# Cluster attention and two gated layers on one core: the product of p and v in one run every second iteration, the fill's steps in the other iterations

## The chip, the cores and the metric

One core of a Trainium2 chip runs the whole program. The metric is the device time of one execution in microseconds (us); the median of the runs counts.

## The reference, cut to what is computed

Attention with 2 batches, 8 heads, 768 tokens and a head dimension of 64; a key counts for a query only if both have the same nearest centroid (of 16). Its output passes through two feed-forward blocks.

```python
q_assign = np.argmax(np.einsum('bhsd,hcd->bhsc', q_n, c_n), axis=-1)
k_assign = np.argmax(np.einsum('bhsd,hcd->bhsc', k_n, c_n), axis=-1)
mask = q_assign[:, :, :, None] == k_assign[:, :, None, :]
scores = np.where(mask, scale * np.matmul(q, k.transpose(0, 1, 3, 2)), -1000000000.0)
attn = np.exp(scores - np.max(scores, axis=-1, keepdims=True))
attn = attn / (np.sum(attn, axis=-1, keepdims=True) + 1e-09)
x = np.matmul(attn, v)                       # (1536, 512) after the heads are joined
x = ((x @ w1) * (x @ w2)) @ w3 @ w_out       # 512 -> 1024 -> 1024 -> 512
h = x @ w_in                                 # 512 -> 2048
out = (np.maximum(h, 0.0) + alpha * np.minimum(h, 0.0)) @ w_out2
```

## The kernel before, in words

The attention is cut into 96 "units": 16 heads (b, h) times 6 tiles of 128 queries. Two neighbouring units form a pair g (48 of them). A software pipeline written out by hand (the loop of L710) runs one iteration per unit; iteration i holds steps of several units:

- `emit_T(i - 4)`: six transposes of the normalised p of unit i-4 on TensorE, into the two buffers of the PSUM tag "t" (L497);
- `emit_S(i + 1)`: four products that make the scores of unit i+1, two of 128 rows (L457) and two of 80 rows that add the mask (L458);
- `emit_x`: takes the finished output o of a pair out of PSUM, half by ScalarE (L527), half by VectorE (L528); `emit_r`: reciprocals of the row sums of a pair on VectorE (L479, L480); `emit_norm(i - 2)`: p times the reciprocal on GpSimd (L483);
- `emit_evac(i - 4)`: the transposes out of PSUM into the tile pt, three by ScalarE (L504), three by VectorE (L505);
- `emit_max(i + 1)`: row maxima on VectorE (L465); `emit_exp(i)`: the exponential on ScalarE (L472);
- `h_split`: once per unit u of six iterations the operands of the next head are prepared: at i = 6u three operations on GpSimd (L416, L417, L421), then a chain of transfers on the SP queue (L427, L429, L431, and the mask rows mk, L435 and L436); the first score product of the next head waits for them;
- one step of the `fill` (a generator of other work). In the first half the fill prepares the masks of the remaining heads (its products are called ja, jb, jc, jd and je); from iteration 56 a step is 12 products of 384 columns (called l1a and l1b) of the first feed-forward layer for batch 0. With a fill step go steps of the weight conversion (`w_goal`): three operations on VectorE (L181, L182, L185), then a cast on ScalarE (L226) and a subtraction on GpSimd (L227). Before the change a fill step runs in every iteration below 24, between 41 and 55 and from 96 on, and otherwise in even iterations;
- `emit_PV(g, part)`: the product of p and v of pair g. The two units of the pair go to two column halves of the array (tile positions (0, 0) and (0, 64)), each 64 columns wide, while all other products of the loop but ja use the full 128 columns. Three of the six key tiles are done in iteration 2g+6, three in 2g+7; in the trace each half is a run of 12 matmul records (each fp32 product is two records), that is 6 records side by side on the two halves. The PSUM tag "o" has one buffer, so the product of the next pair waits until `emit_x` has emptied it.

After the loop come the rest of the first layer for batch 0, then batch 1, and the remaining layers.

On every engine the order of instructions is that of the code (`manual_schedule`), and each engine waits in order.

Of the kernel before, what the change touches and what calls it, by code (L numbers as in the profile page):

```python
# [17 lines left out]
P = 128  # L18
NT = S // P
# [9 lines left out]
def kernel(  # L29
# [221 lines left out]
    def pst(tag, shape, name, bufs=1):  # L251
        return ps.tile(shape, F32, tag=tag, name=name, bufs=bufs)
# [151 lines left out]
    def h_split(u, j):  # L404

        if u >= B * H:
            return
        b, h = divmod(u, H)
        if j == 0:
            ST[u] = st_tile(f"st{u}")  # L410
        s, r = ST[u], hraw.get(u)
        f = f32(s)
        pool = u % 2 == 1 or 0 < u < 9
        if j == 0:
            if pool:
                nc.gpsimd.tensor_scalar(out=r, in0=r, scalar1=qsc, scalar2=1.0, op0=ALU.mult, op1=ALU.mult)  # L416
            nc.gpsimd.tensor_scalar(  # L417
                out=s[:, 3], in0=r, scalar1=1.0 if pool else qsc, scalar2=1.0, op0=ALU.mult, op1=ALU.mult
            )
            if pool:  # L420
                nc.gpsimd.tensor_tensor(out=s[:, 1], in0=r, in1=f[:, 3], op=ALU.subtract)  # L421
            else:
                nc.vector.scalar_tensor_tensor(
                    out=s[:, 1], in0=r, scalar=qsc, in1=f[:, 3], op0=ALU.mult, op1=ALU.subtract
                )
        elif j == 1:
            nc.sync.dma_start(out=f[0:64, 0:4:2], in_=f[64:128, 3:4].to_broadcast([64, 2, S]))  # L427
        elif j == 2:
            nc.sync.dma_start(out=f[64:128, 0], in_=f[64:128, 1])  # L429
        elif j == 3:  # L430
            nc.sync.dma_start(out=f[64:128, 1], in_=f[0:64, 3])  # L431
        elif j == 4:
            mk = MK[b, h // 4].rearrange("p a b -> p (a b)")
            hl = h % 4
            nc.sync.dma_start(out=f[64:80, 2], in_=mk[16 * hl : 16 * hl + 16])  # L435
            nc.sync.dma_start(out=f[64:80, 3], in_=mk[64 + 16 * hl : 64 + 16 * hl + 16])  # L436
        else:
            hraw.pop(u)
            h_load(u + 1)


    NU = B * H * NT
    scp, pt, sums, pth, ob, XR = {}, {}, {}, {}, {}, {}

    def unit(i):
        return i // NT, i % NT

    def emit_S(i):
        if i >= NU:
            return  # L450
        u, qt = unit(i)
        s = ST[u]
        t = pst("s", [P, 2, 512], f"s{i}", bufs=2)
        q = slice(qt * P, qt * P + P)
        for a in range(2):
            ks = slice(a * HS, a * HS + HS)
            nc.tensor.matmul(t[:, a, 0:HS], lhsT=s[:, 0, q], rhs=s[:, 1, ks], start=True, stop=False)  # L457
            nc.tensor.matmul(t[:, a, 0:HS], lhsT=s[0:80, 2, q], rhs=s[0:80, 3, ks], start=False, stop=True)  # L458
        scp[i] = t
# [3 lines left out]
    def emit_max(i):  # L463
        m = ap.tile([P, 1], F32, tag="nmax", bufs=3, name=f"nm{i}")
        nc.vector.tensor_reduce(out=m, in_=scp[i][:, :, 0:HS], op=ALU.max, axis=AX.XY, negate=True)  # L465
        nmax[i] = m

    def emit_exp(i):
        if i % 2 == 0:
            sums[i // 2] = ap.tile([P, 2], F32, tag="sums", bufs=3, name=f"su{i}")  # L470
        p = ap.tile([P, S], F32, tag="p", bufs=6, name=f"p{i}")
        nc.scalar.activation(  # L472
            out=p.rearrange("p (a k) -> p a k", a=2), in_=scp.pop(i)[:, :, 0:HS], func=AF.Exp,
            bias=nmax.pop(i), scale=1.0, accum_out=sums[i // 2][:, i % 2 : i % 2 + 1],
        )
        pt[i] = p

    def emit_r(g):
        nc.vector.tensor_scalar(out=sums[g], in0=sums[g], scalar1=1e-9, scalar2=None, op0=ALU.add)  # L479
        nc.vector.reciprocal(out=sums[g], in_=sums[g])  # L480

    def emit_norm(i):
        nc.gpsimd.tensor_scalar(  # L483
            out=pt[i], in0=pt[i], scalar1=sums[i // 2][:, i % 2 : i % 2 + 1], scalar2=1.0, op0=ALU.mult, op1=ALU.mult
        )
# [3 lines left out]
    def emit_T(i):  # L489
        g, j = divmod(i, 2)  # L490
        if j == 0:
            pth[g] = ap.tile([P, NT, 256], F32, tag="pth", bufs=3, name=f"pt{g}")
        for a in range(2):
            t = pst("t", [P, 3, P], f"t{i}{a}", bufs=2)
            for k in range(3):
                kt = 3 * a + k
                nc.tensor.transpose(t[:, k], pt[i][:, kt * P : kt * P + P], ident)  # L497
            tps[i, a] = t
        pt.pop(i)

    def emit_evac(i):
        g, j = divmod(i, 2)
        q = slice(j * P, j * P + P)
        nc.scalar.copy(out=pth[g][:, 0:3, q], in_=tps.pop((i, 0)))  # L504
        nc.vector.tensor_copy(pth[g][:, 3:6, q], tps.pop((i, 1)))  # L505

    def emit_PV(g, part):

        u, qt = unit(2 * g)
        if part == 0:  # L510
            ob[g] = pst("o", [P, P], f"o{g}")
        v = VS[u // 2]
        for kt in range(3 * part, 3 * part + 3):
            for j in range(2):
                nc.tensor.matmul(  # L515
                    ob[g][64 * j : 64 * j + 64], lhsT=v[:, u % 2, kt], rhs=pth[g][:, kt, j * P : j * P + P],
                    start=(kt == 0), stop=(kt == NT - 1), tile_position=(0, 64 * j),
                )

    def emit_x(g):  # L520
        u, qt = unit(2 * g)
        o = ob.pop(g)
        p = u // 2
        if u % 2 == 0 and qt == 0:
            XR[p] = cp.tile([P, S], F32, tag=f"xr{p % 4}", name=f"xr{p}")
        mine = slice(0, 64) if u % 2 == 0 else slice(64, 128)
        nc.scalar.copy(out=XR[p][mine, qt * P : qt * P + P], in_=o[0:64])  # L527
        nc.vector.tensor_copy(XR[p][mine, qt * P + P : qt * P + 256], o[64:128])  # L528
        pth.pop(g)
# [17 lines left out]
    def x_split(b, p, a):  # L547
        if b not in XS:
            XS[b] = cp.tile([P, 8 * S], F32, tag="wox", name=f"xs{b}").bitcast(F32R).rearrange("p (t k s) -> p t k s", t=2, k=4)
        r = XR[4 * b + p]  # L550
        s = slice(a * HS, a * HS + HS)
        nc.scalar.copy(out=XS[b][:, 0, p, s], in_=r[:, s])
        pool = a if b == 1 else 1 - a
        (nc.gpsimd if pool else nc.vector).tensor_tensor(out=XS[b][:, 1, p, s], in0=r[:, s], in1=f32(XS[b][:, 0, p, s]), op=ALU.subtract)
# [25 lines left out]
    with tc.manual_schedule():  # L580
# [126 lines left out]
        LT = 4  # L707
        L1_B, L1_D = 16, 24
        NUH = NU // 2
        for i in range(NU + 9):  # L710
            if 0 <= i - LT < NU:
                emit_T(i - LT)
            if i + 1 < NU:
                emit_S(i + 1)

            g2 = i - 8
            if g2 >= 0 and g2 % 2 == 0 and g2 // 2 < NU // 2:
                emit_x(g2 // 2)
            if i >= 2 and i % 2 == 0 and i // 2 - 1 < NU // 2:
                emit_r(i // 2 - 1)  # L720
            if 0 <= i - 2 < NU:
                emit_norm(i - 2)
            if 0 <= i - LT < NU:
                emit_evac(i - LT)
            if i + 1 < NU:
                emit_max(i + 1)
            if i < NU:
                emit_exp(i)
                u, j = unit(i)
                for k in ((0,), (1, 2), (3,), (4,), (5,), ())[j]:  # L730
                    h_split(u + 1, k)
            if i >= NU or i % 2 == 0 or i < 24 or 40 < i < 56:
                if fill_at[0] < (L1_B if i < NU else L1_D):
                    if next(fill) is not None:
                        fill_at[0] += 1
            if NUH + 4 <= i < NUH + 8:
                x_split(0, i - NUH - 4, 0)
                x_split(0, i - NUH - 4, 1)
                xdone.append(i)
            if i == NU - 1:  # L740
                late.append(i)
                for k in range(2):
                    w = st_tile(f"wo{k}").rearrange("p a n -> p (a n)").rearrange("p (g t n) -> p g t n", g=3, t=2)
                    for g in range(3):
                        WO[3 * k + g] = w[:, g, 0], w[:, g, 1]
            if i >= NU - 1:
                w_goal(at["wo", 0, 3, 0])

            k = i - 6
            if k >= 0 and k // 2 < NU // 2:  # L750
                emit_PV(k // 2, k % 2)
                if k % 12 == 11:
                    v_load(k // 12 + 2)
        pscope.close()

# [178 lines left out]
```

## Time and profile before

| what | us |
|---|---|
| runs before | 808.74, 809.0, 2352.5; median 809.0 |
| the profiled execution's own time | 809.13 |
| its span, first to last instruction | 807.0 |
| busy in it: PE (matmul) | 769.3 (95%) |
| busy in it: DVE | 496.5 (62%) |
| busy in it: ACT | 393.7 (49%) |
| busy in it: POOL | 244.7 (30%) |

One of the three runs lies far off and does not move the median. The span is 2.1 us shorter than the execution's own time. PE, DVE, ACT, POOL and SP are TensorE, VectorE, ScalarE, GpSimd and the engine that issues transfers. A matmul's duration in the trace is its latency: neighbouring records overlap, so what a product costs is the distance between starts.

### The profile page before, as it was taken

Reading aid. Unit: us, or ns where it says so; the run is one execution under the profiler, and the core shown is the slowest. Engines: PE = TensorE matmul, PEld = TensorE weight load, DVE = VectorE, ACT = ScalarE, POOL = GpSimd, SP = SyncE. Lnnn points to the kernel's source line nnn. Section 1 sums busy time; section 2 is a strip of 40 time slices with the busy share of each in tenths; the row PEclk is TensorE's granted clock in tenths of the full one; section 3 lists DMA queues with packets and bytes.
Section 4 is the critical chain, followed back from the end, with each engine's and each line's share of the span. In section 5 each row is a group of like instructions: output and inputs, shape, how many; then the busy total and the mean of one; then the engine's idle time right before and its main releaser. Section 6 shows DMA issues by size and latency. Waiting matters only on the chain.

```text
span 807.0 us, 13411 instructions
## 1 busy us (share of the span) xinstructions
PE 769.3 (95%) x5073; PEld 679.6 (84%) x5073; DVE 496.5 (62%) x836; ACT 393.7 (49%) x836; POOL 244.7 (30%) x222
## 2 busy tenths in 40 slices
PE   4799999799999999969999999999999999999998
PEld 2667888678888888959998899999999878999996
DVE  3866888987878777785545599334456663323222
ACT  5677766665555564543233345334544554323232
POOL 0465456566464534243222243001112220000000
PEclk9999999999999999979999999999999999999999
DMA  7555344545545517546444498025665738333332
GB/s 250 175 160 175 76 107 101 139 98 158 161 147 139 165 55 213 188 172 225 161 137 160 154 310 276 39 79 167 212 191 187 225 115 287 131 120 121 126 131 78
DMA packets 38863, 127.31 MB, mean 158 GB/s; under 512 B 5168, under 2 KB 5296, under 8 KB 38800
## 3 DMA queue, kind: packets, MB, share of 16 engines
q1 hardware_dynamic: 38800, 126.46, 50.0%
q8 instruction: 40, 0.66, 0.3%
q14 instruction: 23, 0.19, 0.1%
HBM read 84.08 MB, written 28.31 MB: 139 GB/s over the span
## 4 chain that ended last, share of the span: by engine, by line
PE 84%; DVE 6%; ACT 3%; issue 3%; DMA 2%; POOL 1%; SPq 1%; POOLq 0%; ACTq 0%; DVEq 0%
PE o L515 9%; PE t L497 8%; PE l L246 8%; PE l L244 8%; PE l L245 7%; PE acc L246 5%; PE acc L245 5%; PE acc L244 5%; PE s L457 4%; PE s L458 4%; PE l1a L245 3%; PE l1a L244 3%; PE l1a L246 3%; PE l1b L244 2%; PE l1b L245 2%
## 5 line engine op out<-in xcount | busy, mean ns | idle before, releaser
L227 POOL TENSOR_TENSOR wh<-wt,wh 128x512 fp32r<-128x512 f32 x64 | 86.5, 1352 | 239.0 <-DVE g L852 119.6
L483 POOL TENSOR_SCALAR p<-p,su 128x768 f32<-128x768 f32 x96 | 91.3, 958 | 125.8 <-DVE su L480 64.2
L848 DVE SCALAR_TENSOR_TENSOR gr<-gr,alp 128x384 f32<-128x384 f32 x64 | 41.7, 651 | 107.3 <-ACT gr L847 107.3
L465 DVE TENSOR_REDUCE nm<-s 128x1 f32<-128x768 f32 x96 | 91.5, 953 | 9.9 <-PE s L458 6.3
L472 ACT ACTIVATE p<-s,nm 128x768 f32<-128x768 f32 x96 | 87.0, 906 | 6.2 <-DVE nm L465 6.2
L515 PE MATMUL o<-pt,vs 128*64 128x128 f32 x1152 | 84.6, 282 | 5.3 <-DVE xr L528 5.3
L497 PE MATMUL t<-cst,p 128*128 128x128 f32 x576 | 85.2, 283 | 1.7 <-DVE pt L505 1.7
L515 PEld LDWEIGHTS o<-pt,vs 128*64 128x64 f32 x1152 | 61.4, 137 | 29.4 <-issue 18.3
L457 PE MATMUL s<-st 128*128 128x384 f32 x192 | 74.4, 387 | 3.4 <-ACT p L472 3.3
L497 PEld LDWEIGHTS t<-cst,p 128*128 128x128 f32 x576 | 61.6, 141 | 18.8 <-issue 13.1
L246 PE MATMUL acc<-wh,g 128*128 128x512 f32 x192 | 75.3, 392 | 0.0
L244 PE MATMUL acc<-wh,g 128*128 128x512 f32 x192 | 74.8, 390 | 0.6 <-ACT os L872 0.6
L245 PE MATMUL acc<-wh,g 128*128 128x512 f32 x192 | 75.3, 392 | 0.0
L504 ACT COPY pt<-t 128x384 f32<-128x384 f32 x96 | 46.0, 479 | 53.4 <-PE t L497 52.9
L846 ACT ACTIVATE gr<-l 128x384 f32<-128x384 f32 x64 | 31.2, 487 | 82.3 <-PE l L246 82.3
L182 DVE SCALAR_TENSOR_TENSOR wt<-wr,wt 128x512 uint32<-128x512 uint32 x72 | 68.1, 945 | 2.5
L505 DVE COPY pt<-t 128x384 f32<-128x384 f32 x96 | 53.3, 555 | 26.4 <-PE t L497 24.9
L458 PE MATMUL s<-st 80*128 80x384 f32 x192 | 66.1, 344 | 1.8 <-DMA st<-mk 1.8
L185 DVE SCALAR_TENSOR_TENSOR wt<-wu,wt 128x512 uint32<-128x512 uint32 x72 | 61.5, 854 | 2.5
L851 ACT CAST g<-gr 128x384 fp32r<-128x384 f32 x64 | 32.8, 513 | 59.6 <-DVE gr L848 59.6
L852 DVE TENSOR_TENSOR g<-gr,g 128x384 fp32r<-128x384 f32 x64 | 35.7, 558 | 37.1 <-ACT g L851 37.1
L226 ACT CAST wh<-wt 128x512 fp32r<-128x512 f32 x64 | 39.7, 620 | 38.5 <-DVE wt L185 20.0
(132 smaller groups left out, 1786.9 us busy)
## 6 DMA issues: line engine op xcount, KB each, us to landing
wh<-kept SPq DMA_DIRECT2D x58, 512.0 KB, 3.5
wr<-in_w_dram SPq DMA_DIRECT2D x48, 512.0 KB, 5.0
kept<-wh SPq DMA_DIRECT2D x48, 512.0 KB, 5.5
wr<-in_w3t_dram SPq DMA_DIRECT2D x16, 512.0 KB, 4.3
jm<-in_qka_dram SPq DMA_DIRECT2D x12, 512.0 KB, 5.4
hr<-in_qkh_dram SPq DMA_DIRECT2D x16, 384.0 KB, 3.4
st<-st SPq DMA_DIRECT2D x16, 384.0 KB, 3.7
st<-st SPq DMA_DIRECT2D x32, 192.0 KB, 2.6
```

The costliest lines, as they stand in the source:

```text
L182: nc.vector.scalar_tensor_tensor(out=t, in0=r[:, :, 0], scalar=29, in1=t, op0=ALU.logical_shift_right, op1=ALU.bitwise_or)
L227: nc.gpsimd.tensor_tensor(out=lo, in0=tts.pop(n), in1=f32(hi), op=ALU.subtract)
L244: nc.tensor.matmul(o, lhsT=whi, rhs=xhi, start=first, stop=False)
L245: nc.tensor.matmul(o, lhsT=whi, rhs=xlo, start=False, stop=False)
L246: nc.tensor.matmul(o, lhsT=wlo, rhs=xhi, start=False, stop=last)
L457: nc.tensor.matmul(t[:, a, 0:HS], lhsT=s[:, 0, q], rhs=s[:, 1, ks], start=True, stop=False)
L458: nc.tensor.matmul(t[:, a, 0:HS], lhsT=s[0:80, 2, q], rhs=s[0:80, 3, ks], start=False, stop=True)
L465: nc.vector.tensor_reduce(out=m, in_=scp[i][:, :, 0:HS], op=ALU.max, axis=AX.XY, negate=True)
L472: nc.scalar.activation(out=p.rearrange("p (a k) -> p a k", a=2), in_=scp.pop(i)[:, :, 0:HS], func=AF.Exp, bias=nmax.pop(i), scale=1.0, acc ...
L483: nc.gpsimd.tensor_scalar(out=pt[i], in0=pt[i], scalar1=sums[i // 2][:, i % 2 : i % 2 + 1], scalar2=1.0, op0=ALU.mult, op1=ALU.mult)
L497: nc.tensor.transpose(t[:, k], pt[i][:, kt * P : kt * P + P], ident)
L515: nc.tensor.matmul(ob[g][64 * j : 64 * j + 64], lhsT=v[:, u % 2, kt], rhs=pth[g][:, kt, j * P : j * P + P], start=(kt == 0), stop=(kt == N ...
```

## The change

`emit_PV` loses its argument `part` and does all six key tiles of a pair in one run at the end of iteration 2g+6 (even); iterations 2g+7 hold no product of p and v. `emit_x` of pair g moves from iteration 2g+8 (even) to 2g+7 (odd), still the first one after the product is complete. Where the fill had the even iterations only (24 to 40, 56 to 95) it has the odd ones; steps and their number stay, and each comes one iteration later. The load of the next v (L402) is issued one iteration earlier. The loop ends one iteration sooner.

```diff
-    def emit_PV(g, part):
+    def emit_PV(g):
 
         u, qt = unit(2 * g)
-        if part == 0:
-            ob[g] = pst("o", [P, P], f"o{g}")
+        ob[g] = pst("o", [P, P], f"o{g}")
         v = VS[u // 2]
-        for kt in range(3 * part, 3 * part + 3):
+        for kt in range(NT):
...
-        for i in range(NU + 9):
+        for i in range(NU + 8):
...
-            g2 = i - 8
-            if g2 >= 0 and g2 % 2 == 0 and g2 // 2 < NU // 2:
-                emit_x(g2 // 2)
+            if i >= 7 and i % 2 == 1 and (i - 7) // 2 < NU // 2:
+                emit_x((i - 7) // 2)
...
-            if i >= NU or i % 2 == 0 or i < 24 or 40 < i < 56:
+            if i >= NU or i % 2 == 1 or i < 24 or 40 < i < 56:
...
-            if k >= 0 and k // 2 < NU // 2:
-                emit_PV(k // 2, k % 2)
-                if k % 12 == 11:
+            if k >= 0 and k % 2 == 0 and k // 2 < NU // 2:
+                emit_PV(k // 2)
+                if k % 12 == 10:
                     v_load(k // 12 + 2)
```

On TensorE, around the first step of the first layer, the order before is: transposes (t), scores (s), 12 products l1a, half a product of p and v (o), transposes, scores, the other half, transposes.

```order
L246 MATMUL l1a_2209<-xs_2065,wh_1926 128x384
L515 MATMUL o_2233<-pt_2109,vs_1673 64x128 x6
L497 MATMUL t_2240<-cst,p_2095 128x128 x3
L497 MATMUL t_2244<-cst,p_2095 128x128 x3
L457 MATMUL s_2248<-st_1922 128x384
L458 MATMUL s_2248<-st_1922 128x384
L457 MATMUL s_2248<-st_1922 128x384
L458 MATMUL s_2248<-st_1922 128x384
L515 MATMUL o_2233<-pt_2109,vs_1673 64x128 x6
L497 MATMUL t_2269<-cst,p_2133 128x128 x3
```

The order at the same place of the changed kernel, where emit_PV's line is L514:

```order
L246 MATMUL l1a_2246<-xs_2065,wh_1963 128x384
L497 MATMUL t_2271<-cst,p_2133 128x128 x3
L497 MATMUL t_2275<-cst,p_2133 128x128 x3
L457 MATMUL s_2279<-st_1912 128x384
L458 MATMUL s_2279<-st_1912 128x384
L457 MATMUL s_2279<-st_1912 128x384
L458 MATMUL s_2279<-st_1912 128x384
L514 MATMUL o_2296<-pt_2184,vs_1646 64x128 x12
L497 MATMUL t_2309<-cst,p_2176 128x128 x3
```

The run of o between l1a and t is gone, and the next one is 12 products long instead of 6.

On VectorE, around the first two weight conversions (wt), the order before has each of them in an odd iteration (47 and 49), with the copy of o (xr) and the reciprocals (su) of the following even iteration behind it.

```order
L465 TENSOR_REDUCE nm_1952<-s_1944 128x1
L181 TENSOR_SCALAR wt_1960<-wu_1888 128x512
L182 SCALAR_TENSOR_TENSOR wt_1960<-wr_120,wt_1960 128x512
L185 SCALAR_TENSOR_TENSOR wt_1960<-wu_1888,wt_1960 128x512
L528 COPY xr_1763<-o_1929 64x128
L479 TENSOR_SCALAR su_1919<-su_1919 128x2
L480 RECIPROCAL su_1919<-su_1919 128x2
L505 COPY pt_1972<-t_1977 128x3x128
```

In the changed kernel the conversions stand in the even iterations 48 and 50, and behind each comes xr of the odd iteration; this is the first of them.

```order
L479 TENSOR_SCALAR su_1840<-su_1840 128x2
L480 RECIPROCAL su_1840<-su_1840 128x2
L505 COPY pt_1888<-t_1893 128x3x128
L465 TENSOR_REDUCE nm_1907<-s_1897 128x1
L181 TENSOR_SCALAR wt_1920<-wu_1918 128x512
L182 SCALAR_TENSOR_TENSOR wt_1920<-wr_118,wt_1920 128x512
L185 SCALAR_TENSOR_TENSOR wt_1920<-wu_1918,wt_1920 128x512
L527 COPY xr_1731<-o_1926 64x128
L505 COPY pt_1888<-t_1943 128x3x128
```

The reciprocals no longer stand behind xr, and the conversion has moved into the iteration in which GpSimd prepares a head (48 = 6 x 8).

## Rows read from the trace of the kernel before

**Rows 1.** Stretch, length, busy PE, PEld, DVE, ACT, POOL, granted clock, DMA share, GB/s
```profile
116.00:147.00 31.00, 30.61 (x291) 25.30 (x288) 27.18 (x52) 20.27 (x48) 18.54 (x19) 1.00 0.42 105
147.00:177.40 30.40, 23.73 (x206) 19.30 (x205) 26.85 (x42) 20.06 (x47) 20.20 (x19) 0.94 0.40 110
177.40:300.00 122.60, 122.60 (x1032) 105.92 (x1032) 99.43 (x173) 70.43 (x158) 60.90 (x59) 1.00 0.49 140
```

**Rows 2.** Waits of PE: engine, line, waited for, us in total, times, longest
```profile
PE o L515 <- DVE xr L528: 5.3, 3, 4.0
PE s L458 <- DMA st<-mk: 1.8, 1, 1.8
```

**Rows 3.** Timeline of PE in order of start: one half product and its neighbours
```profile
256.29 0.33 PE L458 MATMUL s<-st 80*128 80x384 f32 x1
256.55 0.88 PE L515 MATMUL o<-pt,vs 128*64 128x128 f32 x12
257.36 0.88 PE L497 MATMUL t<-cst,p 128*128 128x128 f32 x6
257.99 0.42 PE L457 MATMUL s<-st 128*128 128x384 f32 x1
258.25 0.34 PE L458 MATMUL s<-st 80*128 80x384 f32 x1
```

**Rows 4.** Timeline cut to records in flight at 256.9, at 257.2 and at 257.7
```profile
256.71 0.50 PE L515 MATMUL o<-pt,vs 128*64 128x128 f32 x6
...
256.93 0.50 PE L515 MATMUL o<-pt,vs 128*64 128x128 f32 x6
...
257.53 0.38 PE L497 MATMUL t<-cst,p 128*128 128x128 f32 x2
```

**Rows 5.** Timeline of PE: scores followed at once by transposes, without a product between
```profile
32.63 0.87 PE L497 MATMUL t<-cst,p 128*128 128x128 f32 x6
...
36.99 0.34 PE L458 MATMUL s<-st 80*128 80x384 f32 x1
37.17 0.49 PE L352 MATMUL jd<-cst,jm 128*128 128x128 f32 x3
37.50 0.82 PE L497 MATMUL t<-cst,p 128*128 128x128 f32 x6
38.07 0.42 PE L457 MATMUL s<-st 128*128 128x384 f32 x1
```

**Rows 6.** Timeline of the SP queue: last mask transfer of unit 5
```profile
100.02 0.54 SPq L436 DMA_DIRECT2D st<-mk  x1
```

**Rows 7.** Timeline of PE: the first two score products of unit 5
```profile
102.03 0.42 PE L457 MATMUL s<-st 128*128 128x384 f32 x1
102.37 0.41 PE L458 MATMUL s<-st 80*128 80x384 f32 x1
```

**Rows 8.** Timeline of DVE: the first two weight conversions and what follows each
```profile
149.11 0.43 DVE L181 TENSOR_SCALAR wt<-wu 128x512 uint32<-128x512 uint32 x1
...
151.02 0.29 DVE L528 COPY xr<-o 64x128 f32<-64x128 f32 x1
...
154.66 2.03 DVE L181 TENSOR_SCALAR wt<-wu 128x512 uint32<-128x512 uint32 x1
...
159.70 0.29 DVE L528 COPY xr<-o 64x128 f32<-64x128 f32 x1
```

**Rows 9.** Timeline of POOL: longest step of a head's preparation, beside the second conversion
```profile
154.57 1.83 POOL L421 TENSOR_TENSOR st<-hr,st 128x768 fp32r<-128x768 f32 x1
```

**Rows 10.** Timeline of PE: the half product that waits behind the second conversion
```profile
160.05 0.88 PE L515 MATMUL o<-pt,vs 128*64 128x128 f32 x12 [3.98 <-DVE xr L528]
```

**Rows 11.** Timelines of PE and DVE: transposes of iteration 89, evacuated by VectorE
```profile
286.81 0.88 PE L497 MATMUL t<-cst,p 128*128 128x128 f32 x6
...
287.73 0.56 DVE L505 COPY pt<-t 128x384 f32<-128x384 f32 x1 [0.65 <-PE t L497]
```

**Rows 12.** Page, costliest groups: the maxima on VectorE, busy us and mean ns
```profile
L465 DVE TENSOR_REDUCE nm<-s 128x1 f32<-128x768 f32 x96 | 91.5, 953 | 9.9 <-PE s L458 6.3
```

## Prediction

> **What bounds the kernel now.** I began with the busy times by stretch. From 177 to 300 us, where the attention runs with layer-one steps as its fill, TensorE is busy all of the time (122.60 of 122.60 us), and from 116 to 147 us it is busy 30.61 of 31 [rows 1]. So what TensorE no longer does there ends the stage earlier, as long as no other engine takes over. The one stretch where it is not the bound is 147 to 177 us: PE is busy 23.73 of 30.40 us, VectorE 26.85 of 30.40 [rows 1]. I then read PE's waits: in the attention the largest is for VectorE's copy xr, 5.3 us in three pieces, the longest 4.0; one more is for the mask transfer, 1.8 us [rows 2]. Last I read PE's timeline record by record, because the change takes away no arithmetic: only the distances between starts can shrink.
>
> **What a visit to the narrow form costs.** "Visit" means that TensorE goes from full-width products to the 64-column product of p and v and back. Before, each pair g makes two visits, now one. One visit [rows 3, 4]: the last score product starts at 256.29, the first record of o at 256.55, 0.26 later; where scores are followed by a full-width transpose the distance is 0.18 (36.99 to 37.17) [rows 5]. Toll 0.08. The records of o start in pairs. The second pair starts at 256.71, 0.16 after the first; the fourth at 256.93, so inside the run a pair costs (256.93 - 256.71) / 2 = 0.11. Toll 0.05. The six records from 256.93 are pairs four to six, so the last starts at 257.15, and the transposes at 257.36, 0.21 later instead of 0.11. Toll 0.10. The second transpose starts at 257.53, 0.17 after the first; transposes that follow others keep (0.82 - 0.27) / 5 = 0.11, where 0.27 is what one takes beyond the last start [rows 5]. Toll 0.06. Sum 0.29 us. A check: six transposes after o last 0.63 to the next scores (257.36 to 257.99), without o before them 0.57 (37.50 to 38.07) [rows 3, 5].
>
> What comes in its place, scores or l1 directly before the transposes, stands only once with the same tiles: the run at 32.63 lasts 0.87 instead of 0.82 [rows 5], so 0.05 of the toll stays there, perhaps because p had only just come. Bounds: 0.24 to 0.29 per visit. I take 0.29, since jd at 37.17 is a full-width transpose behind scores, as t will be, and paid nothing.
>
> The Trainium skill, TensorEngine Tiling (Array Packing), Key Properties under Tiling Modes, says that going from one tiling mode to another drains TensorE. The trace agrees, with its 0.29 us for both ways; the page gives no price.
>
> **The sum.** 48 visits go (odd iterations 7 to 101): 48 x 0.29 = 13.9 us. Two of these runs stood behind ja, a 32-column product, whose own change of form stays; I take off 0.3. Gross 13.6 us. Not all of it reaches the end:
> - Unit 2 (iterations 7, 9, 11): its scores already wait 1.8 us for the mask transfer [rows 2], so 3 x 0.29 = 0.87 only lengthens that wait. The chain of that transfer begins at GpSimd's preparation, which stands behind the reciprocals; these no longer stand behind xr, which takes 0.29 us (151.02) [rows 8]. Given back 0.2, lost 0.7.
> - Unit 5 (iterations 25, 27, 29): the second score product starts 0.34 after the first (102.03, 102.37) where 0.26 is usual [rows 7, 3]: it was held by the transfer issued at 100.02 [rows 6], 2.35 us before. No slack, so the same loss less the same 0.2 and 0.1 of rounding: 0.6.
> - The stretch of VectorE (iterations 45 to 55, six visits): 6 x 0.29 = 1.7 lost, since VectorE's work there stays the same.
> - Iterations 88 to 95 have no fill: two runs of transposes follow each other with only scores between, 0.57 + 0.80 = 1.37 us from start to start (38.07 - 37.50, and four score products at 0.26, 0.18, 0.18 and 0.18) [rows 3, 5]. VectorE ends the evacuation 1.48 after the start (286.81; 287.73 + 0.56) [rows 11], and its buffer is wanted at 1.37 + 0.33 = 1.70. That leaves 0.2 us; the exponential behind the same evacuations is about as near. I take 0.08 for each of four odd iterations, 0.3 in all.
>
> Left: 13.6 - 0.7 - 0.6 - 1.7 - 0.3 = 10.3 us.
>
> **The moved steps.** xr now has a full iteration before the next product of p and v needs its buffer, so the wait for xr [rows 2] should go as such. But behind it VectorE is late, and the transposes wait for VectorE's evacuation instead: xr, two small operations and the evacuation follow each other. Of the two short pieces (5.3 - 4.0 = 1.3) I give half, 0.6. The long piece [rows 10] belongs to the second conversion, which took 159.70 - 154.66 = 5.04 us beside GpSimd's head preparation [rows 9], where the first took 151.02 - 149.11 = 1.91 [rows 8]. After the change the first conversion stands in iteration 48, beside that preparation, and the second in 50, clear of it: I let the two swap their prices, net 0. Bounds: both at 5.04, 3.1 us more; both at 1.91, 3.1 less.
>
> The fill's steps in odd iterations cost PE the same 12 products. From 56 on, the conversion's cover is one fill step, the transposes and scores of the next iteration and a full product of p and v: 12 x 0.18 + 0.57 + 0.80 + 0.81 + 6 x 0.11 = 5.0 us [rows 3 to 5], about as much as before, so I cost it at nothing; if the cover fails, the third rival below. SP gets the load of v one iteration earlier, behind a product that PE has reached anyway; v is used more than six iterations later: nothing. The iteration that the loop loses held no attention step; its one conversion step is done in the next phase, where VectorE has room: nothing.
>
> Gain 10.3 + 0.6 = 10.9 us. Profiled execution: 809.13 (span 807.0 and 2.1 around it) - 10.9 = 798.2. The median of the runs shown, 809.0, is 0.1 lower, so 798.1; I say 798.
>
> **The rivals.**
> - VectorE becomes the bound early. From 116 to 147 us it is busy 27.18 of 31.00, 88% [rows 1]; two iterations without fill take PE 2 x (0.26 + 0.81 + 0.63 + 0.26 + 0.18 + 0.18) = 4.64 us [rows 3, 5], and 0.29 less is 6%, which makes it 93%; odd and even iterations load it unevenly. Against it: PE has hardly waited for it there so far. Then what is saved from iteration 24 to 55 is lost and only 13 to 23 (6 visits, 1.7 - 0.3) and 57 to 101 (23 visits, 6.7 - 0.3) count: 7.8, so 801.
> - Conversion against head preparation. The rows show that an operation of VectorE beside GpSimd's grew from 0.43 to 2.03 us [rows 8, 9]. If the first conversion now takes 5.04 and the second still does, the stretch is 3.1 us longer: gain 7.8, 801 too. By the SBUF — State Buffer page of the Trainium skill, Who interferes with whom, VectorE instructions with two SBUF inputs contend with GpSimd for a shared port; the trace's growing conversion agrees.
> - Slower than before: conversions in the layer-one stage. There are eight, two of four fill steps having one. If, now in odd iterations, each takes 5.04 beside GpSimd, VectorE needs from the scores' end 0.95 for the maxima [rows 12], 5.04, 0.29 for xr's share and 0.56 for the evacuation [rows 8, 11], and half of the time another 0.56 for layer one, estimated as the like evacuation: 7.1 against a cover of 5.0, so 2.1 us per conversion, 17 in all; where PE stops so long the clock falls, 1.8 us in the stretch of rows 1, at perhaps half of the eight: 7. Then 24 - 11 = 13 us slower than before, 822. It decides from about 3 us per conversion. Against it: the head preparation falls into even iterations there, so fewer conversions should meet it, not more.
> - The waits for xr really go, and with them the clock loss: from 147 to 177 us the granted clock is 0.94, full speed being 2.4 GHz, half of it 1.2; 0.06 x 30.4 = 1.8 us [rows 1]. Then 10.9 + (5.3 - 0.6) + 1.8 = 17.4, so 792.
> - The change doesn't do what it says: the toll belongs to any weight load behind another product, and scores before transposes pay it as well. Only the 32.63 run speaks for that, with 0.05 of 0.29. Gain 0 to 1: 808.
>
> **How the numbers follow.** Forecast (797 to 800) 0.58; the first two rivals together 0.22; waits and clock gone 0.13; no toll saved 0.04; slower 0.03. Two per cent, about what a measurement of this kernel can tell from no change, is 16.2 us: faster means below 792.8, slower above 825.2. The fourth rival, with its own scatter, reaches below 792.8 in most cases: 0.12. The slower rival passes 825.2 only if the clock falls as well: 0.03 at most with everything unforeseen. Same: 0.85. The toll at 0.24 would give 48 x 0.05 = 2.4 less; with the conversions' 3.1 either way the forecast's own range is 794 to 803. The range that leaves out 2 in 10 is 791 to 804.
>
> **What would show it.** In the changed profile: 48 runs of 24 records in place of 96 of 12; scores to transposes 0.18, and a run of o that takes 0.81 + 6 x 0.11 = 1.47 to the next transposes; 4.35 instead of 4.64 us per two iterations without fill; the wait for xr gone; a longer wait for the mask transfer in units 2 and 5; the attention's last o about 11 us earlier, and everything behind it unchanged. Wrong would be: the pair of iterations not shorter by 0.29, a wait of the transposes for VectorE in the layer-one stage, or a later phase that gives time back.

## The result, and where the time went

The changed kernel takes 797.76 us (median of 4 runs, 795.99 to 800.22), the kernel before 808.74, 809.0 and 814.46 in the runs beside them; the ratio is 0.9845 with a 95% interval of 0.9828 to 0.9863. That is faster by 1.4 to 1.7%, less than the 2% that count as a difference here. A fourth run of the kernel before, 2352.5 us, was slow and is left out of the ratio. 798 was forecast. A profiled execution of 795.99 us (span 793.6) stands for it below; its granted clock was 0.989.

First the windows that answer to [rows 1] (columns as there). The first two begin 3 us earlier; the second ends, as there, where TensorE becomes busy without a break, and is 33.6 us long instead of 30.4:

```profile
113.00:144.00 31.00, 29.54 (x292) 25.97 (x289) 27.24 (x51) 20.64 (x49) 18.84 (x19) 1.00 0.48 122
144.00:177.60 33.60, 26.75 (x226) 23.39 (x225) 28.39 (x48) 21.73 (x51) 21.91 (x20) 0.85 0.41 107
177.60:291.50 113.90, 113.90 (x1008) 105.29 (x1008) 87.85 (x166) 67.73 (x155) 55.88 (x56) 1.00 0.52 145
```

The layer-one stage still has TensorE busy all of the time. In the first stretch TensorE now idles 1.46 of 31 us where it idled 0.39. The middle stretch is still VectorE's (busy 28.39 of 33.60 us), and its granted clock is 0.85 instead of 0.94.

Inside the layer-one stage, PE's timeline shows two neighbouring iterations, the first with the product at its end and the second with a fill step instead (its scores and 12 products are cut here); it answers to [rows 3]:

```profile
243.95 0.34 PE L246 MATMUL l1a<-xs,wh 128*128 128x384 f32 x1
244.12 0.82 PE L497 MATMUL t<-cst,p 128*128 128x128 f32 x6
244.70 0.42 PE L457 MATMUL s<-st 128*128 128x384 f32 x1
...
245.32 0.34 PE L458 MATMUL s<-st 80*128 80x384 f32 x1
245.59 1.53 PE L514 MATMUL o<-pt,vs 128*64 128x128 f32 x24
247.05 0.88 PE L497 MATMUL t<-cst,p 128*128 128x128 f32 x6
247.68 0.42 PE L457 MATMUL s<-st 128*128 128x384 f32 x1
...
250.56 0.82 PE L497 MATMUL t<-cst,p 128*128 128x128 f32 x6
```

The run of o takes 247.05 - 245.59 = 1.46 (1.47 forecast). Transposes behind l1a start 0.17 after it and take 0.58 to the scores; behind o they take 0.63. The pair of iterations takes 250.56 - 244.12 = 6.44 us. Before, two iterations with a fill step took 6.75: the transposes of iterations 76 and 80 start at 243.85 and 257.36, which is 13.51 for two pairs. So 0.31 us per pair went, 0.29 of it forecast.

In iterations 88 to 95, which have no fill, scores stand directly before transposes:

```profile
289.21 0.34 PE L458 MATMUL s<-st 80*128 80x384 f32 x1
289.39 0.82 PE L497 MATMUL t<-cst,p 128*128 128x128 f32 x6
```

The distance is 0.18, as forecast, and the pair of iterations from 276.29 to 280.64 takes 4.35, as forecast; before, it took 4.63.

PE's waits over the whole execution, the largest of them that touch the change (columns as in [rows 2]):

```profile
PE t L497 <- DVE pt L505: 7.2, 3, 3.8
...
PE l1a L244 <- ACT xs L551: 2.6, 1, 2.6
...
PE l1a L244 <- DMA wh<-kept: 1.9, 1, 1.9
```

The 5.3 us for xr [rows 2] are gone, and 7.2 us for VectorE's evacuation stand in their place (1.7 before). The waits of l1a, with a third of 1.0 for VectorE's xs, belong to the passage from batch 0 to batch 1 of the first layer. There the kernel before waited 3.93 for pl and 4.02 for xs.

To see where the 13.4 us between the two spans (807.0 and 793.6) came from, I took the start of the first transpose of an iteration in both traces. The forecast's terms are set beside each stage (visits by 0.29 us, less the losses that it named there):

| from, to | start before | start after | gained in the stage | by the forecast's terms |
|---|---|---|---|---|
| iteration 24 | 89.11 | 85.88 | 3.2 | 1.6 |
| iteration 42 | 133.34 | 129.56 | 0.6 | 2.0 |
| iteration 58 | 182.82 | 179.79 | -0.8 | 1.2 |
| iteration 96 | 302.31 | 293.55 | 5.7 | 5.2 |
| first product lc, after layer one | 381.64 | 368.16 | 4.7 | 0.9 |

The total came out as forecast, and its parts did not. One stage is right, two gave less, and the end gave almost 4 us that I had not counted. Behind the first product lc nothing changed: 425.4 us to the end in both traces. Every row compares two single executions. In e1, a second profile of the changed kernel, the rows read 0.6, 0.6, -1.6, 5.7 and 3.0, so the second and fourth hold and the others vary. About half of the first row is luck; the section on the hardware comes back to it.

### The profile page after: what moved, and what is told of

Read it like the earlier page. It is cut to its first block, busy times and chain, and to the rows that moved or that the text cites. A ratio compares the mean times of both kernels' runs of the same rounds, so it can differ in the third digit from the quotient of the medians.

```text
span 793.6 us, 13443 instructions
## 1 busy us (share of the span) xinstructions
PE 757.4 (95%) x5073; PEld 684.5 (86%) x5073; DVE 491.3 (62%) x836; ACT 392.8 (49%) x836; POOL 241.8 (30%) x222
## 4 chain that ended last, share of the span: by engine, by line
PE 82%; DVE 6%; DMA 3%; ACT 3%; issue 3%; POOL 2%; SPq 1%; POOLq 0%; ACTq 0%; DVEq 0%
PE o L514 8%; PE l L246 8%; PE l L244 8%; PE l L245 8%; PE t L497 7%; PE acc L246 5%; PE acc L245 5%; PE acc L244 5%; PE s L458 4%; PE s L457 4%; PE l1a L244 3%; PE l1a L246 3%; PE l1a L245 3%; PE l1b L244 2%; PE l1b L246 2%
## 5 line engine op out<-in xcount | busy, mean ns | idle before, releaser
L483 POOL TENSOR_SCALAR p<-p,su 128x768 f32<-128x768 f32 x96 | 89.2, 939 | 103.3 <-DVE su L480 49.8
L497 PE MATMUL t<-cst,p 128*128 128x128 f32 x576 | 83.3, 280 | 8.2 <-DVE pt L505 7.2
L497 PEld LDWEIGHTS t<-cst,p 128*128 128x128 f32 x576 | 65.0, 142 | 20.2 <-DVE pt L505 8.1
L514 PE MATMUL o<-pt,vs 128*64 128x128 f32 x1152 | 75.4, 281 | 0.0
L514 PEld LDWEIGHTS o<-pt,vs 128*64 128x64 f32 x1152 | 63.7, 140 | 12.9 <-issue 12.9
L182 DVE SCALAR_TENSOR_TENSOR wt<-wr,wt 128x512 uint32<-128x512 uint32 x72 | 70.0, 972 | 2.5
L185 DVE SCALAR_TENSOR_TENSOR wt<-wu,wt 128x512 uint32<-128x512 uint32 x72 | 58.1, 808 | 2.5
```

The costliest lines, as they stand in the source:

```text
L182: nc.vector.scalar_tensor_tensor(out=t, in0=r[:, :, 0], scalar=29, in1=t, op0=ALU.logical_shift_right, op1=ALU.bitwise_or)
L483: nc.gpsimd.tensor_scalar(out=pt[i], in0=pt[i], scalar1=sums[i // 2][:, i % 2 : i % 2 + 1], scalar2=1.0, op0=ALU.mult, op1=ALU.mult)
L514: nc.tensor.matmul(ob[g][64 * j : 64 * j + 64], lhsT=v[:, u % 2, kt], rhs=pth[g][:, kt, j * P : j * P + P], start=(kt == 0), stop=(kt == N ...
```

## The experiments

Ratios are to the kernel before, run beside each; e1 to e4, e5 to e8 and e9 to e10 shared a chip. The kernel before had a median of 810.4, 810.6 and 810.3 us there.

**e1: the changed kernel again**, as the yardstick for the others.

> The changed kernel once more, as the control of this set. If the gain has the parts that its first profile shows (about 8 us up to the last product of p and v, about 4 us at the change from batch 0 to batch 1 of the first layer), the second profile shows both again, and the time is 796 to 800. If the second part was scatter of that one execution, the first product of batch 1 comes only about 9 us earlier than in the kernel before, and the time is near 801.

798.24 us (795.92 to 800.87), ratio 0.9849 [0.9820, 0.9879]. The waits are those of the first profile: 7.1 us for the evacuation, 2.6 and 2.1 at the change of batches.

**e2: the changed kernel with the lost iteration given back; e3: the kernel before with one iteration less.**

```diff
-        for i in range(NU + 8):
+        for i in range(NU + 9):
```

> The changed kernel with the loop one iteration longer, as before the change; that iteration holds no attention step, only one more step of the weight conversion. Theory: this step shifts the conversions by half a pair, so that one stands ahead of the subtractions xs at the change of batches again; 3 to 4 us slower than the control, 800 to 802. Rival: what came after the attention is scatter or follows from the earlier start; the same as the control within 1 us.

> The kernel before with its loop one iteration shorter and nothing else changed. Theory: 3 to 4 us faster than the kernel before, ratio about 0.995 to 0.996, with the wait at the change of batches shortened and no difference up to the last product of p and v. Rival (scatter): ratio 1.000.

e2: 800.95 us, ratio 0.9884 [0.9852, 0.9915], 2.7 slower than e1. e3, the opposite edit on the kernel before: 807.69 us, 0.9961 [0.9948, 0.9974], 2.7 faster than its neighbour. Both ways the length of the loop is worth 2.7 us, where I had cost it at nothing. The interval of e2 overlaps that of e1; that of e3 stays clear of 1, and the traces put the difference in one place: from iteration 96 to the first product lc e2 takes 2.0 us more than e1, and e3 3.5 less than the kernel before. The PE waits of e2 at the change of batches (timeline, last column wait and releaser) say why:

```profile
343.61 0.69 PE L244 MATMUL l1a<-xs,wh 128*128 128x384 f32 x1 [3.95 <-DVE pl L779]
348.32 0.69 PE L245 MATMUL l1a<-xs,wh 128*128 128x384 f32 x1 [4.02 <-DVE xs L553]
```

And the same two products in the changed kernel:

```profile
338.15 0.45 PE L244 MATMUL l1a<-xs,wh 128*128 128x384 f32 x1 [2.55 <-ACT xs L551]
339.57 0.69 PE L245 MATMUL l1a<-xs,wh 128*128 128x384 f32 x1 [0.98 <-DVE xs L553]
```

VectorE's timeline in e2 (the view ends within xs, behind three of its four operations), and then in the changed kernel, shows what stands ahead of xs:

```profile
344.45 0.41 DVE L181 TENSOR_SCALAR wt<-wu 128x512 uint32<-128x512 uint32 x1
...
345.63 1.37 DVE L185 SCALAR_TENSOR_TENSOR wt<-wu,wt 128x512 uint32<-128x512 uint32 x1
346.93 3.90 DVE L553 TENSOR_TENSOR xs<-xr,xs 128x384 fp32r<-128x384 f32 x3
```
```profile
337.89 0.55 DVE L575 TENSOR_TENSOR pr<-l1b,asb 128x384 f32<-128x384 f32 x1
338.35 4.20 DVE L553 TENSOR_TENSOR xs<-xr,xs 128x384 fp32r<-128x384 f32 x4
```

A conversion is done in two half steps: the three operations on VectorE in one call, the cast and the subtraction in the next. One loop iteration less is one half step less, so all later steps change sides. With 105 iterations VectorE's half falls right ahead of xs, for which TensorE has nothing else to do; with 104 it doesn't.

**e4: the changed kernel, its product in two halves again**, the first between the transposes and the scores of the same iteration, so that two visits to the narrow form come back and all else stays.

```diff
+            if k >= 0 and k % 2 == 0 and k // 2 < NU // 2:
+                emit_PV(k // 2, 0)
             if i + 1 < NU:
                 emit_S(i + 1)
...
-                emit_PV(k // 2)
+                emit_PV(k // 2, 1)
```

> The changed kernel with the product of a pair in two halves of the same even iteration, one between the transposes and the scores and one behind the scores: arithmetic, fill, copies of o and loop length as in the changed kernel, but two visits to the narrow form per pair again. Theory (the toll is the gain): TensorE pays 48 x 0.29 = 13.9 us more, of which 8 to 11 reach the end: 806 to 809. Rival (the gain is the earlier copy of o and the shifted fill): within 2 us of the control.

806.97 us, ratio 0.9965 [0.9945, 0.9986], 8.7 slower than e1 and within 0.7 of e3. PE's timeline shows the second visit:

```profile
243.96 0.82 PE L497 MATMUL t<-cst,p 128*128 128x128 f32 x6
244.71 0.88 PE L515 MATMUL o<-pt,vs 128*64 128x128 f32 x12
245.51 0.44 PE L457 MATMUL s<-st 128*128 128x384 f32 x1
...
246.41 0.88 PE L515 MATMUL o<-pt,vs 128*64 128x128 f32 x12
247.22 0.88 PE L497 MATMUL t<-cst,p 128*128 128x128 f32 x6
...
250.75 0.82 PE L497 MATMUL t<-cst,p 128*128 128x128 f32 x6
```

The pair takes 250.75 - 243.96 = 6.79 us instead of 6.44. So the toll is paid by the visit, and with scores behind o instead of transposes it is 0.35 rather than 0.31. From iteration 58 to 96, 6.5 of the 8.7 us arise. And e4, with the copies of o and the fill in their new places, is as fast as e3, which has them in the old ones, with the same loop and as many visits: without the merge these moves gain nothing that can be told.

**e5: the changed kernel with the fill back in the even iterations; e6: the kernel before with the fill in the odd ones.**

```diff
-            if i >= NU or i % 2 == 1 or i < 24 or 40 < i < 56:
+            if i >= NU or i % 2 == 0 or i < 24 or 40 < i < 56:
```

> The changed kernel with the fill's steps back in the even iterations (24 to 40 and 56 to 95), where the whole product of p and v also stands. The visits stay one per pair. Theory (the toll is the gain, the parity of the fill only keeps the other engines covered): TensorE's work is the same, but odd iterations shrink to 1.37 us and the transposes behind them meet VectorE's and ScalarE's evacuation; 0 to 4 us slower than the changed kernel, 798 to 802. Rival (the parity carries the gain): back near the kernel before, 806 or more.

> The kernel before with only the fill moved to the odd iterations; two half products per pair, copies of o where they were, loop of 105. Theory: no visit less, so the same as the kernel before within 2 us, ratio 0.998 to 1.003; the first conversion falls beside GpSimd's head preparation in iteration 48 and takes about 4.3 us, the second about 1.9. Rival (parity): 6 us faster or more, ratio 0.992 or less.

e5: 804.58 us, ratio 0.9924 [0.9900, 0.9948], 6.3 slower than e1. That is between the theory's 802 and the rival's 806: more than I expected, though half of the gain stays. e6: 811.01 us, 0.9996 [0.9983, 1.0009]: in the kernel before the parity is worth nothing, although the first two conversions swap their prices there (4.3 and 2.2 us). In e5 VectorE's timeline shows a conversion of the layer-one stage beside the preparation of a head, and PE's what it costs:

```profile
234.69 1.03 DVE L181 TENSOR_SCALAR wt<-wu 128x512 uint32<-128x512 uint32 x1
...
236.99 2.19 DVE L185 SCALAR_TENSOR_TENSOR wt<-wu,wt 128x512 uint32<-128x512 uint32 x1
...
239.53 0.56 DVE L505 COPY pt<-t 128x384 f32<-128x384 f32 x1
```
```profile
238.49 0.49 PE L497 MATMUL t<-cst,p 128*128 128x128 f32 x3
240.15 0.55 PE L497 MATMUL t<-cst,p 128*128 128x128 f32 x3 [1.17 <-DVE pt L505]
```

The three operations take 236.99 + 2.19 - 234.69 = 4.49 us, VectorE's evacuation comes late, and the second run of three transposes waits 1.17. Three of the eight conversions in the stage are such; they cost 3.5 us of waits. In the kernel before the like conversions took 4.2 us and cost about 0.1 each: its odd iteration held half a product between the scores and the next transposes, 0.80 us long, which gave VectorE that much more time. The merged product leaves that iteration with scores alone, and this cover is gone. In the changed kernel the same three conversions take 2.8 and five take 1.9, and the trace lists no wait of PE from 190 to 290 us. So the move of the fill does not gain by itself; it keeps the merge from giving back half of what it gains. These waits are 3.5 of the 4.9 us that e5 loses against e1 from iteration 58 to 96; the rest of the 6.3 was not traced.

**e7: the changed kernel with one fill step more, in iteration 24**, which puts the two conversions ahead of the layer-one stage into iterations 47 and 49.

```diff
-            if i >= NU or i % 2 == 1 or i < 24 or 40 < i < 56:
+            if i >= NU or i % 2 == 1 or i < 25 or 40 < i < 56:
```

> The changed kernel with one more fill step in iteration 24, so that all later steps up to 55 come one iteration earlier and the first two weight conversions stand in iterations 47 and 49 as before the change. Theory (a conversion is slow beside the head preparation of iteration 48): the first takes 1.9, the second 4 to 5 us, the sum as in the changed kernel, and the time the same within 1.5 us. Rival (their iteration alone does not matter, only VectorE's other work): both 2 to 3 us.

799.52 us, ratio 0.9850 [0.9827, 0.9874]: the same as e1. The conversions swap their prices back; the second begins with

```profile
152.29 2.07 DVE L181 TENSOR_SCALAR wt<-wu 128x512 uint32<-128x512 uint32 x1
```

The two take 1.9 and 5.1 us. The transposes then wait 2.6 for GpSimd's p and 0.7 for the evacuation in place of 3.8.

**e8: two pairs in one run, every fourth iteration**, with a tile o of twice the size.

```diff
-        ob[g] = pst("o", [P, P], f"o{g}")
+        if g % 2 == 0:
+            ob["t"] = pst("o", [P, 2, P], f"o{g}")
+        ob[g] = ob["t"][:, g % 2]
...
-            if k >= 0 and k % 2 == 0 and k // 2 < NU // 2:
+            if k >= 2 and k % 4 == 2 and k // 2 < NU // 2:
+                emit_PV(k // 2 - 1)
                 emit_PV(k // 2)
```

> The changed kernel carried one step further: the products of two pairs in one run every fourth iteration, so 24 visits instead of 48; copies of o for both pairs one iteration later. Theory: another 24 x 0.29 = 7.0 us less on TensorE, of which about two thirds reach the end, as with the first 48: 4 to 5 us faster than the changed kernel, 793 to 794, less up to 2 us where three iterations without a product follow each other at 1.37 us and meet the evacuations. Rival (the gain came from the even and odd balance, which this spoils): slower than the changed kernel.

814.48 us, ratio 1.0042 [1.0025, 1.0059]: 0.4% slower than the kernel before, where a gain was expected. What TensorE saves, it loses in the bare iterations. PE's timeline in the layer-one stage:

```profile
252.00 2.84 PE L516 MATMUL o<-pt,vs 128*64 128x128 f32 x48
254.77 0.88 PE L497 MATMUL t<-cst,p 128*128 128x128 f32 x6
...
258.31 0.82 PE L497 MATMUL t<-cst,p 128*128 128x128 f32 x6
...
260.07 0.85 PE L497 MATMUL t<-cst,p 128*128 128x128 f32 x6 [0.23 <-ACT pt L504]
```

The run of 24 products takes 254.77 - 252.00 = 2.77 us where two of 12 take 2.92, so it saves. But the bare iteration from 258.31 to 260.07 takes 1.76 us where its six transposes and four score products need 1.37 by the forecast's own sum, and so four iterations take 13.25 us on average (24 of them from 210.81 to 290.29) instead of 12.88. Ahead of the stage the transposes wait 5.4 us for ScalarE and 6.2 for VectorE, and that is the larger part: against e1's trace e8 loses 6.9 us from iteration 24 to 58 and 2.2 from there to 96.

**e9: the changed kernel with the fill steps of iterations 48 and 49 done in 38 and 40**, so that both conversions stand clear of a head's preparation; **e10: the same with the step of 38 done in 24.**

```diff
-            if i >= NU or i % 2 == 1 or i < 24 or 40 < i < 56:
+            if i >= NU or (i % 2 == 1 or i < 24 or 37 < i < 56) and i not in (48, 49):
```

> The changed kernel with the fill's steps of iterations 48 and 49 moved to 38 and 40, so that the first two weight conversions stand in iterations 46 and 50, both away from the preparation of a head (42, 48, 54). Theory (a conversion beside the preparation is what makes the transposes wait for VectorE's evacuation): both conversions take about 1.9 us, the wait of 3.8 us in that stretch goes, so do some 0.8 us at the half clock behind it, and the time is 3 to 5 us below the changed kernel: 793 to 795. Rival (the stretch is VectorE's sum of work, wherever the conversions stand): VectorE saves 2.4 us of its 4.3, at most that reaches the end, and the waits turn up in the neighbouring iterations: 796 to 798.

> As the run before it, but the fill's step of iteration 38 is done in iteration 24. In the run that took the step of 24 alone the stretch of iterations 28 to 42 was about 1.3 us shorter, with the waits for the mask preparation gone. Theory (head and mask preparation hold units 5 to 8): both gains add, 1 to 1.5 us below the run before it: 792 to 794. Rival (the pipeline of heads has its own length, whatever the fill): the same time as the run before it within 0.5 us.

e9: 796.35 us (795.40 to 797.42), ratio 0.9828 [0.9814, 0.9843]; e10: 796.37 us (792.89 to 798.49), 0.9814 [0.9784, 0.9844]. Both lie 1.9 us below e1, but all three intervals overlap, so neither is shown to beat the changed kernel. The time of e9 lies in the rival's range, 796 to 798, at its lower edge, and not in the theory's 793 to 795; that of e10 is also the rival's, the same as e9. The trace of e9 shows the waits of the stretch on PE's timeline:

```profile
150.30 0.55 PE L497 MATMUL t<-cst,p 128*128 128x128 f32 x3 [1.13 <-DVE pt L505]
...
161.39 0.55 PE L497 MATMUL t<-cst,p 128*128 128x128 f32 x3 [2.14 <-DVE pt L505]
...
173.36 0.77 PE L497 MATMUL t<-cst,p 128*128 128x128 f32 x3 [2.62 <-DVE pt L505]
```

The conversions took 2.3 and 2.6 us, beside GpSimd's normalisation of p, and a wait of 1.1 is left behind the first. These waits sum to 5.9 us where the changed kernel has 6.8, so most of the stall is not the preparation's. That the rest is VectorE's sum of work between two runs of transposes fits, but no run tests it alone. The stretch from iteration 42 to 58 took 47.7 us instead of 50.2; two fill steps had left it, and its granted clock was 0.96 instead of 0.90. In e10 iterations 28 to 42 took 32.3 us instead of 33.5 in the changed kernel, and that didn't show in the median.

## Why the prediction came out right, and where its parts were wrong

**Right: the toll per visit.** 0.29 us was put together from distances between starts [rows 3 to 5]; the layer-one stage gained 0.31 per pair, and e4, which undoes this alone, gave 8.7 us back. The rival by which scores before transposes pay the toll as well falls: scores to transposes take 0.18 in iterations 88 to 95, and behind l1a the transposes take 0.58 to the scores, within 0.01 of what they took without o. For these 19 visits the forecast was 5.2, and 5.7 was measured. The 0.3 that I took off for VectorE in iterations 88 to 95 was not lost (4.35 to 4.38 us for each pair).

**Right: xr's wait turns into one for the evacuation.** Of the 5.3 us nothing is left, and the evacuation has 5.5 more. The 0.6 that I gave back for the short pieces did not come.

**Mis-sized: the stretch of VectorE.** I had its length change by the swap of two conversions at net 0, plus 0.6 for short waits. The swap came as described. In the changed kernel VectorE and GpSimd read:

```profile
148.12 0.89 DVE L181 TENSOR_SCALAR wt<-wu 128x512 uint32<-128x512 uint32 x1
...
150.27 2.17 DVE L185 SCALAR_TENSOR_TENSOR wt<-wu,wt 128x512 uint32<-128x512 uint32 x1
...
156.50 0.41 DVE L181 TENSOR_SCALAR wt<-wu 128x512 uint32<-128x512 uint32 x1
...
157.68 0.69 DVE L185 SCALAR_TENSOR_TENSOR wt<-wu,wt 128x512 uint32<-128x512 uint32 x1
```
```profile
149.78 2.11 POOL L421 TENSOR_TENSOR st<-hr,st 128x768 fp32r<-128x768 f32 x1
```

The first conversion now takes 4.3 us, the second 1.9. But PE waits twice, 3.79 and 3.06 us, 6.8 in all where it waited 6.7 for xr and pt in this stretch before:

```profile
153.41 0.90 PE L497 MATMUL t<-cst,p 128*128 128x128 f32 x3 [3.79 <-DVE pt L505]
...
172.06 0.90 PE L497 MATMUL t<-cst,p 128*128 128x128 f32 x3 [3.06 <-DVE pt L505]
```

Behind each of the two stops the products ran at the lower of the clock's two levels (1.2 GHz instead of 2.4) for a while; the granted clock of these two windows, 0.50 and 0.52, shows it:

```profile
153.00:156.00 3.00, 2.59 (x11) 2.15 (x13) 2.47 (x6) 2.03 (x5) 2.67 (x4) 0.50 0.43 96
172.00:174.00 2.00, 1.94 (x7) 1.68 (x7) 1.97 (x6) 0.99 (x2) 0.96 (x2) 0.52 0.48 106
```

From iteration 42 to 58 the kernel lost 0.8 us, where I had 1.2 of gain. The granted clock of that stretch is 0.90, and 0.97 before; as an estimate from these, 0.10 x 50.2 = 5.0 us are lost to the clock now and 0.03 x 49.5 = 1.5 were before. So the waits were no shorter, and the term that was missing is the clock behind them.

The second stop is not a conversion's. Ahead of it VectorE runs L423, the third operation of head 10's preparation. For the heads 0, 10, 12 and 14 this operation stands on VectorE, not on GpSimd as the list at the top has it:

```profile
168.88 1.75 DVE L423 SCALAR_TENSOR_TENSOR st<-hr,cst,st 128x768 fp32r<-128x768 f32 x1 [0.67 <-POOL st L417]
```

Behind it come a subtraction xs, the copy xr and the evacuation that the transposes wait for. Before, the same L423 (173.64, 1.75 us) cost a wait of 1.41, and xr came behind the evacuation.

**Mis-sized: iterations 24 to 42.** I took losses at unit 5 only, 0.6 of nine visits' 2.6. Unit 5's mask came in time. The loss came in four other places, each a step of the chain that prepares, normalises or masks p:

```profile
87.56 0.45 PE L457 MATMUL s<-st 128*128 128x384 f32 x1 [0.62 <-ACT p L472]
...
108.53 0.87 PE L497 MATMUL t<-cst,p 128*128 128x128 f32 x6 [0.44 <-POOL p L483]
...
114.61 0.41 PE L458 MATMUL s<-st 80*128 80x384 f32 x1 [0.36 <-DMA st<-mk]
...
123.12 0.88 PE L497 MATMUL t<-cst,p 128*128 128x128 f32 x6 [0.22 <-POOL p L483]
```

These sum to 1.64 us, where the kernel before lists no wait of PE from 89 to 132 us, and 0.6 was gained of 2.6. Most of this is the first rival, an engine that becomes the bound early, though the engine named was VectorE, and here ScalarE, GpSimd and a transfer stood last.

**Wrong: "The iteration that the loop loses held no attention step; its one conversion step is done in the next phase, where VectorE has room: nothing."** VectorE has no room at the change of batches: there TensorE waits for it, and e2 and e3 put 2.7 us on the side on which the half step falls. Without this gain, e2 against the kernel before, the change is worth 9.4 us, 1.5 less than the 10.9 forecast; with it, e1 against the kernel before, 12.1. The forecast of 798 is close for two reasons that it did not have. The uncounted gain more than covers what the two stages above lost, and the 809.0 from which I subtracted lies 1.3 to 1.6 below the later medians of the same kernel (810.3 to 810.6), which makes up for the surplus. That the total fits to a fraction of a microsecond is luck; the toll per visit is not.

**The slower rival** had its mechanism right. Conversions beside a head's preparation do hold the transposes of the layer-one stage, as e5 shows, at 1.2 us each for three of eight where I had 2.1 for all. The argument against it, that the fill in odd iterations keeps them clear of the preparation, is the one that held.

## What to carry to other kernels

In this kernel each visit to the narrow form cost 0.31 us, so put the narrow products together, but read first what the shortened iteration covered on other engines: a run twice as long again saved TensorE 0.15 us and cost more in a bare iteration. When a merge takes cover out of every second iteration, move side work to the iteration that keeps it. And count the calls of any generator that is stepped by the loop: one call more or less changes which engine stands ahead of a late wait, here 2.7 us.

## What the runs showed of the hardware

An operation of VectorE beside one of GpSimd reads less as one that runs slower than as one that stands still: L185 of the changed kernel, begun at 150.27, ends at 152.44, and GpSimd's L421 ends at 151.89, 0.55 before; alone L185 takes 0.69. In e7 L181, begun 0.03 us after L421, takes 2.07 us and ends 0.28 behind it. The Trainium skill, SBUF — State Buffer, Who interferes with whom, says of the port that the two share that whichever comes first has it for its whole instruction, and the other one blocks; the traces agree, with those 2.17 and 2.07 us for 0.69 and 0.43. L185 reads two tiles, wu and wt; L181 reads wu alone and was held too, so the two inputs that the prediction names do not cover the row that it sets beside them (0.43 to 2.03).

Single runs of the changed kernel spread over 4.9 us (795.92 to 800.87). Part of this arises at the start of the attention, where TensorE's clock differs. The windows from 48 to 60 us of the first profile of the changed kernel and of e1 differ in the granted clock, 1.00 and 0.86:

```profile
48.00:60.00 12.00, 10.66 (x119) 8.06 (x118) 7.26 (x15) 9.25 (x19) 7.23 (x8) 1.00 0.68 210
```
```profile
48.00:60.00 12.00, 10.30 (x99) 8.18 (x102) 5.74 (x12) 7.70 (x15) 6.85 (x7) 0.86 0.66 207
```

Ahead of it e1's TensorE waited 1.70 us for the mask transfer of unit 2, the other 1.33. Iteration 24 begins at 85.88 in the one and at 88.53 in the other.

More traces tell how much of the 3.2 us in the first line of the table is luck. Seven have the same code up to iteration 24 as the changed kernel (its own, e1, e2, e5, e7, e9 and e10). They begin iteration 24 between 85.88 and 91.38, 88.9 on average, and the profile in the table is the earliest of them. The two whose clock from 48 to 60 us is 1.00 come first, 85.88 and 87.41; the five with 0.86 follow from 88.53 on. Three have the code before (the kernel before, e3 and e6): 89.11 to 91.47, 90.5 on average. As an estimate from these ten traces the change is worth 1.6 us up to there, which is what the forecast's terms give, and the other 1.6 are the luck of one execution. The wait for unit 2's mask, which the forecast let grow by 0.7, is 1.3 to 2.6 us in the seven and 1.7 to 1.9 in the three, so 0.2 more on average. Whether the clock makes the difference or follows from the waits ahead of it was not tested.
